# A linear-attention block: reciprocals of the feature sums applied to the values in place of the features

## The chip, the cores and the metric

The kernel runs on one core of a Trainium2 chip. The metric is the device time of one execution in microseconds (us); lower is better. The time before is the median of three runs. One more execution was taken with the hardware profiler; its trace gives the durations used below. The engines are PE (matrix products), ACT, DVE and POOL (elementwise work), and SP, which issues the DMAs. PEld is PE's loading of weights, beside its products.

## The reference

One block: layer norm, linear attention with 16 heads of 28 channels, projection and residual, then layer norm, a gated unit and residual. B is 1, S 2048, D 448, the gated unit is 1792 wide; inputs and outputs are bfloat16.

```python
def _A_ref(x, wqkv, w_phi, wo):
    ...
    pq = jnp.einsum("bhsd,hdf->bhsf", q, w_phi)
    pk = jnp.einsum("bhsd,hdf->bhsf", k, w_phi)
    phi_q = jnp.concatenate([_softmax(pq, axis=-1), _softmax(-pq, axis=-1)], axis=-1)
    phi_k = jnp.concatenate([_softmax(pk, axis=-1), _softmax(-pk, axis=-1)], axis=-1)
    kv = jnp.einsum("bhsf,bhsd->bhfd", phi_k, v)
    z  = jnp.einsum("bhsf->bhf", phi_k)
    num = jnp.einsum("bhqf,bhfd->bhqd", phi_q, kv)
    den = jnp.einsum("bhqf,bhf->bhq", phi_q, z)[..., None] + 1e-6
    o = num / den
    ...
def _B_ref(x, w_gate, w_up, w_down):
    g = jnp.einsum("bsd,df->bsf", x, w_gate)
    u = jnp.einsum("bsd,df->bsf", x, w_up)
    h = _sigmoid(g) * u
    return jnp.einsum("bsf,fd->bsd", h, w_down)
...
x = A_x
h = x + _A_ref(_layernorm(x, axis=-1), A_wqkv, A_w_phi, A_wo)
h2 = h + _B_ref(_layernorm(h, axis=-1), B_w_gate, B_w_up, B_w_down)
```

What matters here: per token, head and sign, the key features are exponentials divided by their sum over 28 channels. `kv` is the sum over all tokens of features times values, `z` the sum of the features. `kv` and `z` need all 2048 tokens before any query can use them.

## The kernel before

**Tiling.** The 2048 tokens are 16 tiles of 128 (t), eight pairs of tiles (pr) and four groups of 512 tokens for the queries (c). The gated unit goes over chunks of 2, 4, 4, 4 and 2 tiles.

**Order.** Every step is a `task` with a name, an engine or a choice of engines, a function that issues its instructions, and the tasks it depends on. A table of numbers, ORDER, gives the order of all tasks: a number divided by 32 is the task, and the remainder picks the engine and, for matrix products, which PSUM banks they fill. `emit` hands each engine its own in-order queue of instructions with semaphore waits: a task waits for what it depends on and for the readers of what its banks held before. TURNS adds a few more waits. So an instruction that waits holds everything that stands behind it on its engine.

**First stage, weights.** SP loads `x`, and the parts of `wqkv` (L474): `Wv`, the key part, and the query part in four pieces called `wq_raw`. `w_phi` is folded into the key and the query weights on the chip. For the queries, two DMA transposes (L513), each reading two of the four pieces, give `WqT`; PE multiplies it with `Wp` (L569, the fold), and copies bring the result to `Wq`. Copies from PSUM share one helper, so `Wk`, `Wq`, `v`, `xnT`, `oT` and `opm` copies all carry line L438.

**Second stage, keys and values.** Per tile: the statistics of the norm (L597 to L607), `xn` (L614 to L618, on DVE, ACT or POOL; ACT's use a small product `nm`, L607), a transpose to `xnT` (SP's DMA transpose L636, or PE for the first tiles with a copy L438), the key and value products into two PSUM banks (L656), the two exponentials `ek` on ACT, a copy of the values `v` with a column of ones beside each head (L438), the sum over channels (`half_s` L686 and the small reduction L692 for the tiles in SPLIT, one large reduction L697 for the others), the reciprocal `rsum` (L701), the features `phi` = `ek` x `rsum` (L703, 896 elements, on DVE or POOL) and 16 `kv` products (L715) that add up in bank 4. `phi` is padded to 32 columns per head, so a weight load has 64 columns. The ones beside the values make the same products give `z`. A product pair takes one of three pairs of banks, (0,1), (2,3) and (6,7); tiles in VV share: two value products fill one pair, two key products another. Between these, the query products (L755) and their exponentials `eq` (L765) are put in.

**Third stage.** `kvz` (L770) takes bank 4 once all 16 tiles are in. Then, per tile, `num` (L791), a copy `opm` (L438), and per pair the division in small steps on DVE and POOL (`rSm` L807, `rr` L809, `b` L811, `c` L814, `rden` L817, `o` L819), the transpose of `o` (`oT`), the product with `wo` (L852), the residual `h` (L882), the second norm (L886 to L896) and its transpose.

**Fourth stage.** Gate and up products (L953), the sigmoid (L962), their product `hh` (L972), down products (L989), the last residual (L996) and the stores (L999). L1009 are products on a bank that nobody reads, put in where PE would be idle.

Of the kernel before, what the change touches and what calls it, by code (L numbers as in the profile page):

```python
# [10 lines left out]
P = 128  # L11
D = 448
# [319 lines left out]
def build(nc, A_x, A_wqkv, A_w_phi, A_wo, B_w_gate, B_w_up, B_w_down, out):  # L332
# [13 lines left out]
    out_t = out[0].rearrange("(n p) d -> p n d", p=P)  # L346
    wd_v = B_w_down.rearrange("(ft p) n -> p ft n", p=P)

    NXP, NEK, NPHI, NV, NOP, NO, NHP, NSG, NSA = 10, 6, 6, 6, 4, 2, 2, 4, 4
    SPLIT = tuple(range(2, 15))  # L350

    with ExitStack() as es:
# [697 lines left out]
```

## Time and profile before

| what | value |
|---|---|
| runs | 203.47, 203.40, 202.22 us; median 203.4 |
| profiled execution | 202.34 us, first to last instruction 200.6 us |
| granted clock of PE, mean | 1.000 |
| DMA | 16.67 MB in 34052 packets, mean 83 GB/s |

A page of the profile counts, for each engine, the time in which it ran instructions. Matrix products are pipelined, so a busy PE can still be held up. The chain of waits follows the work back from the last instruction, at each step to whatever released it. Groups show a line's instructions with their busy time, the mean of one in ns, and the idle time ahead of them. Windows give, for a stretch of the span, each engine's busy time; the columns are named where they are shown.

### The profile page before, as it was taken

How to read it: one execution, taken by the hardware profiler on the slowest of the kernel's cores; microseconds unless marked ns; L12 is line 12 of the kernel's file. 1: busy time of each engine (PE TensorE's matmuls, PEld its weight loads, DVE VectorE, ACT ScalarE, POOL GpSimd, SP SyncE). 2: the span in 40 equal slices, each digit the busy share in tenths (PEclk: the TensorE clock that was granted, in tenths of full speed). 3: DMA queues.
4: the chain of work that ended last, by engine and by line, in shares of the span. 5: the costliest groups of instructions: out<-in, count | busy, mean ns of one | idle time of the engine just before them, and what ended most of it. 6: DMA issues, size and time to landing. Idle time of an engine off the chain costs nothing.

```text
span 200.6 us, 5433 instructions
## 1 busy us (share of the span) xinstructions
PE 195.1 (97%) x2287; PEld 106.5 (53%) x2287; DVE 130.1 (65%) x295; ACT 93.6 (47%) x167; POOL 51.4 (26%) x80
## 2 busy tenths in 40 slices
PE   7999999997999999999999999999999999999994
PEld 2654555555457884444444444555544445785553
DVE  2999999988989999896746942501243345544042
ACT  2699999799997744324242343000002335442000
POOL 6679475460155682540100100100000000000000
DMA  6985589644140460804520004200024000000014
GB/s 186 355 199 115 147 172 269 176 157 137 40 108 3 98 109 21 184 0 101 117 82 0 0 3 54 52 3 0 0 52 137 3 0 3 2 3 3 23 47 159
DMA packets 34052, 16.67 MB, mean 83 GB/s; under 512 B 25644, under 2 KB 33004, under 8 KB 34028
## 3 DMA queue, kind: packets, MB, share of 16 engines
q1 hardware_dynamic: 33676, 16.04, 31.7%
q8 instruction: 18, 0.29, 0.7%
q10 hardware_dynamic: 352, 0.29, 0.4%
q14 instruction: 6, 0.05, 0.1%
HBM read 8.98 MB, written 1.84 MB: 54 GB/s over the span
## 4 chain that ended last, share of the span: by engine, by line
PE 80%; ACT 12%; DVE 2%; POOL 2%; DMA 2%; issue 1%
PE bank L953 42%; PE bank L989 21%; PE bank L656 9%; ACT eq L765 7%; PE bank L852 4%; ACT opm L438 3%; DMA x_sb<-in_A_x_dram 2%; PE bank L715 1%; PE bank L755 1%; DVE st L597 1%; PE bank L791 1%; ACT v L438 1%; POOL rs L602 1%; ACT ek L678 1%; PE bank L569 0%
## 5 line engine op out<-in xcount | busy, mean ns | idle before, releaser
L953 PE MATMUL bank<-xnT,wg_sb 64*128 64x512 bf16 (+1 forms) x490 | 87.3, 333 | 0.0
L953 PE MATMUL bank<-xnT,wu_sb 64*128 64x512 bf16 (+1 forms) x490 | 87.3, 333 | 0.0
L962 ACT ACTIVATE sg_sb<-bank 128x512 f32<-128x512 f32 (+1 forms) x70 | 34.6, 513 | 81.3 <-PE bank L953 76.3
L972 DVE SCALAR_TENSOR_TENSOR hh<-sg_sb,bank 128x512 bf16<-128x512 f32 (+1 forms) x70 | 38.8, 576 | 29.5 <-ACT sg_sb L962 29.5
L953 PEld LDWEIGHTS bank<-xnT,wg_sb 64*128 64x128 bf16 x490 | 45.6, 94 | 19.1 <-issue 0.8
L953 PEld LDWEIGHTS bank<-xnT,wu_sb 64*128 64x128 bf16 x490 | 45.6, 94 | 18.3
L989 PE MATMUL bank<-wd_sb,hh 128*128 128x448 bf16 (+2 forms) x238 | 42.8, 342 | 0.0
L989 PEld LDWEIGHTS bank<-wd_sb,hh 128*128 128x128 bf16 x238 | 22.5, 98 | 20.3 <-issue 0.4
L996 DVE SCALAR_TENSOR_TENSOR x_sb<-bank,x_sb 128x448 bf16<-128x448 f32 (+2 forms) x17 | 9.7, 594 | 29.7 <-PE bank L989 29.7
L656 PE MATMUL bank<-Wk,xnT 64*128 64x448 bf16 x112 | 20.3, 350 | 0.0
L656 PE MATMUL bank<-Wv,xnT 64*128 64x448 bf16 x112 | 20.0, 350 | 0.1
L765 ACT ACTIVATE eq<-bank 128x1024 bf16<-128x1024 f32 x16 | 16.1, 1058 | 0.1
L755 PE MATMUL bank<-xnT,Wq 64*128 64x512 bf16 x112 | 13.6, 376 | 0.0
L852 PE MATMUL bank<-wo_sb,oT 64*128 64x448 bf16 x112 | 13.1, 349 | 0.3 <-ACT eq L765 0.2
L438 ACT CAST opm<-bank 128x960 bf16<-128x960 f32 x14 | 13.0, 982 | 0.2 <-PE bank L791 0.2
L656 PEld LDWEIGHTS bank<-Wk,xnT 64*128 64x128 bf16 x112 | 8.7, 94 | 6.0 <-DMA xnT<-xn_pad 0.9
L686 POOL TENSOR_TENSOR half_s<-ek 128x448 f32<-128x448 bf16 x10 | 9.7, 977 | 6.7 <-DVE phi L703 2.6
L656 PEld LDWEIGHTS bank<-Wv,xnT 64*128 64x128 bf16 x112 | 8.6, 94 | 4.6 <-ACT ek L678 0.6
L892 POOL TENSOR_TENSOR rs<-rs,neghalf 128x2 f32<-128x2 f32 x8 | 5.6, 700 | 19.1 <-DVE rs L890 13.9
L597 DVE BATCH_NORM_STATS2 st<-x_sb 128x6 f32<-128x448 bf16 x16 | 9.0, 610 | 2.2 <-DMA x_sb<-in_A_x_dram 2.1
L882 DVE TENSOR_TENSOR x_sb<-bank,x_sb 128x896 bf16<-128x896 f32 x8 | 8.7, 1092 | 2.6 <-PE bank L852 2.6
L819 POOL TENSOR_TENSOR o_pad<-b_sb,rden 128x896 bf16<-128x896 bf16 x4 | 6.8, 1688 | 13.1 <-DVE rden L817 13.1
(92 smaller groups left out, 198.0 us busy)
## 6 DMA issues: line engine op xcount, KB each, us to landing
wg_sb<-in_B_w_gate_dram SPq DMA_DIRECT2D x4, 448.0 KB, 3.7
wu_sb<-in_B_w_up_dram SPq DMA_DIRECT2D x4, 448.0 KB, 4.3
out_dram<-x_sb SPq DMA_DIRECT2D x15, 112.0 KB, 1.8
wd_sb<-in_B_w_down_dram SPq DMA_DIRECT2D x7, 224.0 KB, 2.8
x_sb<-in_A_x_dram SPq DMA_DIRECT2D x2, 448.0 KB, 5.6
x_sb<-in_A_x_dram SPq DMA_DIRECT2D x3, 224.0 KB, 4.0
wq_raw<-in_A_wqkv_dram SPq DMA_DIRECT2D x4, 128.0 KB, 4.3
Wv<-in_A_wqkv_dram SPq DMA_DIRECT2D x2, 224.0 KB, 4.3
```

The source lines that it names most:

```text
L438: return e.copy(dst, src) if hasattr(e, "activation") else e.tensor_copy(dst, src)
L597: task(("bst", t), "dve", dve(D), lambda e, t=t: e.bn_stats(st1[:, t % 4, :], X(t)), [x_ld[t], opt(("agg", t - 4))])
L656: r = e.matmul(bank[bk][:, 0:D], lhsT=half(xnT, hi)[:, t, k, :], rhs=half(w, hi)[:, k, :], start=(i == 0), stop=(i == 6), tile_position=(6 ...
L686: task(("sa", t), None, 0.88, lambda e, t=t, s=s: e.tensor_tensor(half_s[:, t % NSA].rearrange("p (a n) -> p a n", a=4 * G), ek[:, s].rear ...
L755: r = e.matmul(bank[bb[j]], lhsT=half(Wq2, hi)[:, k, 2 * g:2 * g + 2].rearrange("p c d h -> p (c d h)"), rhs=half(xnT, hi)[:, 4 * c:4 * c ...
L765: task((key, gp, c), "act", act_p(1024), lambda e, gp=gp, c=c, sg=sg, nm=nm: e.activation(eq[c][:, sg, 2 * gp:2 * gp + 2, :], wide[got(nm) ...
L852: r = e.matmul(bank[bb[j]][:, 0:D], lhsT=half(oT, hi)[:, pr % NO, j, k, :], rhs=half(wo_sb, hi)[:, k, :], start=(i == 0 and not res), stop ...
L953: r = e.matmul(bank[b][:, 0:N], lhsT=half(w, hi)[:, k, fs], rhs=half(hnT, hi)[:, t0:t0 + n, k, :], start=(i == 0), stop=(i == 6), tile_pos ...
L962: task(("sig", f_, c), "act", act_p(N), lambda e, j=j, N=N, nm=nm: e.activation(sg_sb[:, j % NSG, 0:N], bank[got(nm)[0]][:, 0:N], ACT.Tanh ...
L972: task(("hh", f_, c), "dve", dve(N), lambda e, j=j, N=N, nm=nm, f_=f_, c=c: e.scalar_tensor_tensor(hhT[c % NHH][:, f_, 0:N], sg_sb[:, j % ...
L989: r = e.matmul(bank[b][:, c0:c1], lhsT=hhT[c % NHH][:, f_, o:o + P], rhs=wd_sb[:, f_, c0:c1], start=(f_ == 0), stop=(f_ == FT - 1))
L996: task(("fin",) + nm[1:], "dve", dve(c1 - c0), lambda e, nm=nm, tt=tt, pr=pr, c0=c0, c1=c1: e.scalar_tensor_tensor(X(tt)[:, c0:c1], bank[g ...
```

## The change

The features are no longer multiplied by the reciprocals of their sums. Since a reciprocal belongs to one token, head and sign, and `kv` sums over tokens, it can be put on the value side: `vs` holds, for each sign, the values of each head times the reciprocal (28 columns) and the reciprocal itself as the 29th column, which takes the place of the ones. The raw exponentials `ek` are now the weights of the `kv` products, 56 columns at a time. The padded `phi`, its two memsets and the ones go; `ek` has eight slots in place of six, `vs` five. Eight tiles (DIRECT) take the values straight from PSUM on DVE, so their value bank is held until the reciprocals are there; the other eight copy them first (`v1`) and scale them on POOL (tiles 0, 1, 5, 9, 12, 13) or DVE (4, 8). VV and SPLIT have other tiles, and ORDER and TURNS are new throughout.

```diff
-224 0 736 96 544 128 1152 256 480 384 576 28512 608 416 160 28800 640 288 28544 800 320 28576 512 352 768
...
+128 288 0 672 480 1088 384 416 512 28192 544 224 160 28256 576 96 256 28512 448 192 736 28416 704 28448 768
...
-    NXP, NEK, NPHI, NV, NOP, NO, NHP, NSG, NSA = 10, 6, 6, 6, 4, 2, 2, 4, 4
-    SPLIT = tuple(range(2, 15))
+    NXP, NEK, NVS, NV, NOP, NO, NHP, NSG, NSA = 10, 8, 5, 4, 4, 2, 2, 4, 4
+    DIRECT = (2, 3, 6, 7, 10, 11, 14, 15)
+    SPLIT = (2, 4, 5, 6, 7, 8, 10, 11, 12, 13)
...
-        task("v1one", "pool", 0.3, lambda e: e.memset(v1[:, :, :, DH:EV], 1.0))
...
-        VV = (0, 2)
+        VV = (0, 2, 6, 10, 14)
...
+            if t not in DIRECT:
+                task(("v1", t), None, act_p(D), lambda e, t=t: copy(
+                    e, v1[:, t % NV, :], bank[got(v_at[t][0])[v_at[t][1]]][:, 0:D]),
...
-            task(("phi", t), None, 1.68, lambda e, t=t, s=s: e.tensor_tensor(
-                phi[:, t % NPHI, :, :, 0:DH, :].rearrange("p a g d h -> p (a g) d h"),
-                ek[:, s].rearrange("p a (g d h) -> p (a g) d h", g=2 * G, h=2),
...
-                [("rs", t), ("ekp", t), ("ekm", t), opt(("kv", t - NPHI))], engs=("dve", "pool"))
+            task(("rs", t), "dve", dve(256), lambda e, t=t, s=s: e.reciprocal(
+                vs[:, t % NVS, :, :, DH], ssum[:, s, :].rearrange("p (a h) -> p a h", a=2)),
+                [("ss", t), opt(("kv", t - NVS))])
+
+            def scaled(e, t=t):
+                v = bank[got(v_at[t][0])[v_at[t][1]]][:, 0:D] if t in DIRECT else v1[:, t % NV, :]
+                return e.tensor_tensor(
+                    vs[:, t % NVS, :, :, 0:DH], v.rearrange("p (h d) -> p h d", d=DH)[:, None, :, :].to_broadcast([P, 2, H, DH]),
+                    vs[:, t % NVS, :, :, DH:EV].to_broadcast([P, 2, H, DH]), ALU.mult)
+            if t in DIRECT:
+                task(("vs", t), "dve", dve(896), scaled, [("rs", t), v_at[t][2]])
+            else:
+                task(("vs", t), None, 1.68, scaled, [("rs", t), ("v1", t)], engs=("pool", "dve"))
...
-                                         lhsT=phi[:, t % NPHI, sg, 2 * g + hi].rearrange("p d h -> p (d h)"),
-                                         rhs=v1[:, t % NV, h:h + 2, :].rearrange("p h e -> p (h e)"), start=False,
+                                         lhsT=ek[:, t % NEK, sg, (2 * g + hi) * 2 * DH:(2 * g + hi + 1) * 2 * DH],
+                                         rhs=vs[:, t % NVS, sg, h:h + 2, :].rearrange("p h e -> p (h e)"), start=False,
```

The order is read at three places. Lines shift: what was L474, L513, L569 and L636 is L470, L509, L565 and L632 in the changed kernel; L807 to L886 become L814 to L893, L438 becomes L436, and L703, the feature product, becomes L708, the value product.

First, SP's queue around the transposes of the query weights, before, where `in_A_wqkv_dram` is the weight tensor in memory:

```order
L474 DMA wq_raw<-in_A_wqkv_dram 128x4x128
L474 DMA wo_sb<-in_A_wo_dram 64x1x448
L474 DMA wq_raw<-in_A_wqkv_dram 128x4x128 x2
L474 DMA wo_sb<-in_A_wo_dram 80x1x448
L513 DMA_TRANSPOSE WqT<-wq_raw 128x8x128 x2
L636 DMA_TRANSPOSE xnT<-xn_pad 128x8x128 x2
```

And the same place on SP in the changed kernel:

```order
L470 DMA wq_raw<-in_A_wqkv_dram 128x4x128 x3
L470 DMA x_sb<-in_A_x_dram 128x4x448
L470 DMA Wv<-in_A_wqkv_dram 128x2x448
L509 DMA_TRANSPOSE WqT<-wq_raw 128x8x128
L470 DMA wq_raw<-in_A_wqkv_dram 128x4x128
L632 DMA_TRANSPOSE xnT<-xn_pad 128x8x128
L509 DMA_TRANSPOSE WqT<-wq_raw 128x8x128
L470 DMA wo_sb<-in_A_wo_dram 16x1x448
L632 DMA_TRANSPOSE xnT<-xn_pad 128x8x128 x3
```

The last piece of `wq_raw` stood ahead of both transposes and now stands behind the first; a transpose of `xn_pad` has come between the two of `WqT`.

Second, PE's queue where the fold of the query weights with `Wp` stands, before:

```order
L656 MATMUL bank<-Wk,xnT 128x448
L656 MATMUL bank<-Wv,xnT 128x448
L569 MATMUL bank<-Wp,WqT 128x112 x12
L656 MATMUL bank<-Wk,xnT 128x448
L656 MATMUL bank<-Wv,xnT 128x448
```

The same place on PE in the changed kernel:

```order
L656 MATMUL bank<-Wk,xnT 128x448 x8
L656 MATMUL bank<-Wv,xnT 128x448 x6
L656 MATMUL bank<-Wk,xnT 128x448 x6
L565 MATMUL bank<-Wp,WqT 128x112 x4
L656 MATMUL bank<-Wk,xnT 128x448
L656 MATMUL bank<-Wv,xnT 128x448
```

The first group of fold products, which was twelve in one row, is four; the rest follow further on. PE's first products in the whole queue were of values and are now of keys.

Third, DVE's queue ahead of the first residual `h` (written to `x_sb`), before:

```order
L817 RECIPROCAL rden<-b_sb 128x32
L438 COPY oT<-bank 128x512
L811 TENSOR_TENSOR b_sb<-opm,rr 128x928
L819 TENSOR_TENSOR o_pad<-b_sb,rden 128x2x448
L814 TENSOR_TENSOR b_sb<-b_sb,opm 128x928
L838 COPY o_pad<-o_pad 128x2x64
L817 RECIPROCAL rden<-b_sb 128x32
L882 TENSOR_TENSOR x_sb<-bank,x_sb 128x896
L886 BN_STATS st<-x_sb 128x6
```

The same place on DVE in the changed kernel:

```order
L845 COPY o_pad<-o_pad 128x2x64
L818 TENSOR_TENSOR b_sb<-opm,rr 128x928
L436 COPY oT<-bank 128x512
L821 TENSOR_TENSOR b_sb<-b_sb,opm 128x928
L814 RECIPROCAL rSm<-opm 128x32
L824 RECIPROCAL rden<-b_sb 128x32
L816 TENSOR_TENSOR rr<-rSm,opm 128x32
L826 TENSOR_TENSOR o_pad<-b_sb,rden 128x2x448
L845 COPY o_pad<-o_pad 128x2x64
L889 TENSOR_TENSOR x_sb<-bank,x_sb 128x896
L893 BN_STATS st<-x_sb 128x6 x2
L889 TENSOR_TENSOR x_sb<-bank,x_sb 128x896
```

Ahead of the first `h` stand now one more product, `o` of the next pair, with its copy, and the small steps of the pair after it; the second `h` follows the first one's statistics at once.

More of the change, by code (lines that the diff above doesn't have):

```diff
@@ L365, in build @@
         a_0, a_1 = nc.lookup_mloc(ek).addr, nc.lookup_mloc(WkT).addr
[L366 to L367 removed]
+        assert nc.lookup_mloc(xn_pad).addr == a_0 + NEK * 2 * D * 2
         assert nc.lookup_mloc(WqT).addr == a_1 + 3 * KT * D * 2 and KT * P >= D
@@ L676, in build @@
             task(("ekp", t), "act", act_p(D), lambda e, t=t, s=s: e.activation(
-                ek[:, s, 0, :], bank[got(k_at[t][0])[k_at[t][1]]][:, 0:D], ACT.Exp), [k_at[t][2], opt(("phi", t - NEK))])
+                ek[:, s, 0, :], bank[got(k_at[t][0])[k_at[t][1]]][:, 0:D], ACT.Exp), [k_at[t][2], opt(("kv", t - NEK))])
             task(("ekm", t), "act", act_p(D), lambda e, t=t, s=s: e.activation(
                 ek[:, s, 1, :], bank[got(k_at[t][0])[k_at[t][1]]][:, 0:D], ACT.Exp, scale=-1.0),
-                [k_at[t][2], opt(("phi", t - NEK))])
-            task(("v1", t), None, act_p(D), lambda e, t=t: copy(
-                e, v1[:, t % NV, :, 0:DH], bank[got(v_at[t][0])[v_at[t][1]]][:, 0:D].rearrange("p (h d) -> p h d", d=DH)),
-                [v_at[t][2], "v1one", opt(("kv", t - NV))], engs=("act", "dve"))
+                [k_at[t][2], opt(("kv", t - NEK))])
+            if t not in DIRECT:
+                task(("v1", t), None, act_p(D), lambda e, t=t: copy(
+                    e, v1[:, t % NV, :], bank[got(v_at[t][0])[v_at[t][1]]][:, 0:D]),
+                    [v_at[t][2]] + [("vs", u) for u in range(t) if u not in DIRECT and u % NV == t % NV][-1:], engs=("act", "dve"))
             if t in SPLIT:
@@ L689, in build @@
                     ek[:, s].rearrange("p a (g n) -> p (a g) n", g=2 * G)[:, :, DH:2 * DH], ALU.add),
-                    [("ekp", t), ("ekm", t), opt(("ss", t - NSA))],
+                    [("ekp", t), ("ekm", t)] + [("ss", u) for u in SPLIT if u < t and u % NSA == t % NSA][-1:],
                     engs=("pool", "dve"))
@@ L899, in build @@
                     [("rstd2", pr), h_of.get(t)] + [d for d in hT_of.get(pr - NHP, [])])
-            qdone = [("q", gp, c) for gp in range(2)] + [("pb", NT - 1)]
+            qdone = [("q", gp, c) for gp in range(2)] + [k_at[NT - 1][2]]
             if pr in PE_O:
```

27 lines of the change are left out of this document (11 added, 16 removed), and 99 rows, old and new, of tables (ORDER, TURNS).

## The prediction

> **What bounds the kernel now.** The page comes first: span, busy shares, and the chain of waits by engine.
>
> ```profile
> span 200.6 us, 5433 instructions
> PE 195.1 (97%) x2287; PEld 106.5 (53%) x2287; DVE 130.1 (65%) x295; ACT 93.6 (47%) x167; POOL 51.4 (26%) x80
> PE 80%; ACT 12%; DVE 2%; POOL 2%; DMA 2%; issue 1%
> ```
>
> The profiled execution took 202.34 us, 1.74 us more than its span. A busy PE may still be starved, so the chain in order of time comes second.
>
> ```profile
> 24.22 1.13 PE bank L715 x64
> ...
> 33.43 4.65 PE bank L656 x48
> 38.08 0.86 PE bank L755 x8
> ...
> 41.72 4.79 ACT eq L765 x5
> 46.51 4.31 ACT opm L438 x5
> ...
> 61.91 0.23 PE bank L791 x16
> ...
> 62.71 3.49 PE bank L953 x64
> ...
> 123.27 26.59 PE bank L989 x140
> ...
> 181.82 16.05 PE bank L989 x98
> ```
>
> PE carries it up to 39 us, ACT's exponentials and `opm` copies follow, and PE has it again from the first gate/up products (62.7 us) to the end. Third come the windows: per engine its busy time and instructions, then clock, DMA share and GB/s.
>
> ```profile
> 20.00:30.00 10.00, 10.00 (x158) 5.24 (x154) 9.81 (x21) 9.90 (x21) 6.08 (x9) 1.00 0.73 159
> 30.00:39.50 9.50, 9.50 (x177) 5.22 (x174) 9.25 (x20) 8.19 (x18) 4.80 (x5) 1.00 0.83 219
> 39.50:45.00 5.50, 5.48 (x135) 3.16 (x130) 4.67 (x9) 5.47 (x8) 3.33 (x2) 1.00 0.51 170
> 45.00:62.50 17.50, 15.95 (x310) 8.77 (x311) 16.23 (x38) 17.47 (x21) 4.33 (x4) 1.00 0.31 82
> 62.50:90.00 27.50, 27.50 (x414) 17.76 (x412) 26.24 (x72) 12.77 (x27) 15.26 (x13) 1.00 0.36 76
> ```
>
> PE has no gap from 20 to 45 us and none from 62.5 us on; between, 1.55 us are open. The granted clock is 1.00. So two things set the end: when the key/value stage lets `kvz` be formed, and how long after it the gate/up products start. The rest is a fixed row of PE work. DVE (9.81 of 10) and ACT (9.90 of 10) are as full as PE in the first stage, so relief of one alone brings little.
>
> **The change part by part.** *DVE up to `kvz`.* Groups by shape: busy us, mean ns.
>
> ```profile
> L703 DVE TENSOR_TENSOR phi<-ek,rsum 128x896 bf16<-128x896 bf16 x14 | 9.4, 705 | 0.1
> L882 DVE TENSOR_TENSOR x_sb<-bank,x_sb 128x896 bf16<-128x896 f32 x8 | 8.7, 1092 | 2.6 <-PE bank L852 2.6
> L618 DVE TENSOR_SCALAR xn_pad<-x_sb,mv,rs 128x512 bf16<-128x512 bf16 x6 | 2.2, 390 | 0.2 <-POOL rs L602 0.2
> L686 DVE TENSOR_TENSOR half_s<-ek 128x448 f32<-128x448 bf16 x3 | 1.8, 614 | 0.0
> L692 DVE TENSOR_REDUCE ssum<-half_s 128x32 f32<-128x448 f32 x13 | 7.7, 605 | 0.3
> L697 DVE TENSOR_REDUCE ssum<-ek 128x32 f32<-128x896 bf16 x3 | 3.1, 1033 | 0.0
> L438 DVE CAST Wq<-bank 128x448 bf16<-128x448 f32 x1 | 0.6, 614 | 0.0
> L438 ACT CAST v<-bank 128x448 bf16<-128x448 f32 x14 | 7.2, 543 | 0.5 <-PE bank L715 0.4
> L615 ACT ACTIVATE xn_pad<-x_sb,nm,rs 128x512 bf16<-128x512 bf16 x4 | 3.2, 810 | 0.9 <-POOL nm L607 0.9
> ```
>
> Removed: 14 feature products (9.4 us), four `xn` (4 x 0.37 = 1.5), two half sums (1.2), three small reductions that become large ones (3 x 0.59 = 1.8), the `Wq` copy (0.6): 14.5 us. Added: eight products straight from PSUM. The trace has none; the nearest row of the same size that reads PSUM is L882 (1.09 us), the lower bound is the feature product from SBUF (9.4/14 = 0.67). I take 1.09, as it reads the same bank type and count: 8.7 us. Two value products from SBUF on DVE (tiles 4 and 8), between 0.67 and 1.09, middle 0.9: 1.8 us. Three large reductions: 3.1 us; one more `xnT` copy and two tiny `nm` products, 0.6 us by estimate. Sum 14.2, so DVE gains 0.3 us, with ends from a gain of 4.1 (0.67 for all ten) to a loss of 0.1 (1.09 for all ten). It is not relieved. One wait is new: a reciprocal writes into one of five value slots and waits for the `kv` matmuls of the tile five back. Behind it on DVE stand the next sums and products, and PE waits for those. PE issues `kv` of tile 10 ahead of two query groups (28 products at 0.86/8, 3.0 us) and of the last five `kv`, so I cost it at nothing; uncovered it is a part of rival C.
>
> The Trainium skill, "VectorE: DVE Perf Modes", section "The perf-mode tier table (the rule you actually need)", speaks against this edit: a two-tensor operation handles two elements a cycle from bf16 SBUF operands, but one with any PSUM operand. By it (0.96 GHz there) eight products of 896 elements cost an estimated 3.7 us more than the ones removed; by the two rows it is 8 x (1.09 - 0.67) = 3.4 us.
>
> *ACT.* It loses eight value copies (8 x 0.51 = 4.1 us) and gains two `xn` (1.6), one `Wq` copy against one `xnT` copy (nothing): 2.5 us free before its row of `opm` copies. But those need `kvz`, so the gain only waits, unless `kvz` comes earlier. *POOL* takes four more long products and two more `xn`, about 8 us; it was busy 6.08 + 4.80 + 3.33 = 14.2 of 25 us from 20 to 45 us, and the gaps hide them. *PE*: 56 weight columns in place of 64; no row shows a difference, taken as nothing. Two memsets that POOL did during the first loads go, at no gain. The `wd` loads move behind seven more transposes on SP; the first down products stand at 123 us, and the gate/up products ahead of them hide it; without that cover each microsecond of delay would be one of time.
>
> *SP and the fold of the query weights.* The four `wq_raw` pieces went out before the first transposition; now the last piece stands behind it. Issues first, then the times to landing of `wq_raw` and of `WqT`, then the page's busy tenths of DMA.
>
> ```profile
> 8.39 1.13 SPq L474 DMA_DIRECT2D wq_raw<-in_A_wqkv_dram  x2
> ...
> 12.57 3.30 SPq L513 DMA_TRANSPOSE WqT<-wq_raw  x2
> ```
> ```profile
> DMA to landing us min/median/max: 3.2/4.0/4.9
> ```
> ```profile
> DMA to landing us min/median/max: 3.2/3.5/3.7
> ```
> ```profile
> DMA  6985589644140460804520004200024000000014
> ```
>
> The third piece goes out at about 8.4 us as before (12 issues ahead of it, then 13), so the first transposition again starts at 12.6 us and takes half of 3.30. The last piece goes out at 14.2 us. DMA is emptier there (8, then 5 tenths, against 9), so I take its shortest landing, 3.2: 17.4 us. Then the second transposition, 3.5 to landing: 20.9 us (ends 20.6 and 22.8). Who waits is PE, whose fold matmuls need both halves, and behind them the whole row of value and query products. When does PE get there?
>
> ```profile
> 9.09 1.95 ACT L438 CAST Wk<-bank 128x448 bf16<-128x448 f32 x4
> ```
> ```profile
> 10.56 0.93 PE L656 MATMUL bank<-Wv,xnT 64*128 64x448 bf16 x8
> 18.99 0.76 PE L569 MATMUL bank<-Wp,WqT 112*128 112x112 bf16 x12
> ```
>
> Before, PE began with value products at 10.56 us; now it begins with key products, which need the folded `Wk` (copies end at 11.04): 11.2 us, a loss of 0.6. Then come 84 products at 4.65/48 = 0.097 us (8.15) and eight transposes (0.6 by estimate): 19.9 us. It waits 1.0 us (ends 0.6 and 2.9). The transposes of `xn_pad` behind it on SP go out about 1.5 us before PE needs them. As PE has no gap from 20 to 45 us, `kvz` comes 0.6 + 1.0 = 1.6 us later.
>
> *After `kvz`.*
>
> ```profile
> 45.02 0.64 DVE L770 TENSOR_TENSOR kvz<-bank,dmask 128x464 bf16<-128x464 f32 x1 [0.79 <-PE bank L715]
> ...
> 54.52 1.09 DVE L882 TENSOR_TENSOR x_sb<-bank,x_sb 128x896 bf16<-128x896 f32 x1
> ...
> 59.74 1.09 DVE L882 TENSOR_TENSOR x_sb<-bank,x_sb 128x896 bf16<-128x896 f32 x1 [0.39 <-PE bank L852]
> 60.75 0.74 DVE L438 COPY xnT<-bank 128x512 bf16<-128x512 bf16 x2
> ```
>
> Before, `kvz` to the first `h` took 9.5 us, to the end of the `xnT` copies 16.5, to the first gate/up products 17.5 (PE is full from 62.5 on). Five more DVE rows now stand ahead of the first `h`, one product and four small ones, 1.6 us by the sizes above; the second `h` moves ahead of the norm (1.0), where it stood ahead of the copies (1.0). The copies end 18.0 us after `kvz`, the products start at 18.1: 0.6 later. Two more groups of 16 `num` matmuls (0.23 each) are then done ahead of them: 0.5 back. Net 0.1. The tail from the down products on stands in the same order.
>
> Sum: 0.6 + 1.0 + 0.1 = 1.7 us, 202.34 to 204.0. The profiled execution lies 1.1 below the median of the three runs (203.4), so on their scale I forecast 205.1.
>
> **The rivals.** *A, nothing nets (0.25).* The fold is covered: PE is late itself, because ACT (9.90 of 10) frees its banks late. Then the start costs 0.6 at most and the rest 0.1: 203.4 to 204.1, say 203.8. For: the lower end of the wait is only 0.6. Against: the fold needs three DMA steps in a row, and PE had no gap here.
>
> *B, faster (0.10).* DVE is freed of a lock.
>
> ```profile
> L703 DVE TENSOR_TENSOR phi<-ek,rsum x14: 559/615/1385, 21.0 to 43.6; 128x896 bf16<-128x896 bf16 x14
> ```
> ```profile
> 21.32 1.06 POOL L686 TENSOR_TENSOR half_s<-ek 128x448 f32<-128x448 bf16 x1
> ```
>
> The product of 1.385 us ran beside this POOL sum and ended with it; unhindered it takes 0.56. If the PSUM products run free of POOL and near 0.67, DVE gains 4.1 us and this 0.8, and `kvz` comes as soon as PE allows: 224 products at 0.097 (21.7 us), 256 `kv` matmuls at 1.13/64 (4.5), 56 query products at 0.86/8 (6.0), folds and transposes 1.6 by estimate, 33.8 us from 11.2 on, which is 45.0, no earlier than before. What is then left to win is the 1.55 us that PE has open behind it and the 0.46 of the `num` groups: 203.4 - 2.0 = 201.4. It decides if a PSUM product takes under 0.8 us and the chain behind `kvz` fills PE. Against: L882. The Trainium skill, "SBUF — State Buffer", section "Who interferes with whom", says that a DVE instruction with two SBUF inputs contends with a GpSimd instruction that reads SBUF, and one with a single SBUF input outside the two-port modes does not; the PSUM products have one. The 1.385 us agree with the rule.
>
> *C, banks held (0.20).* A value pair must stay in PSUM until two sums, two reciprocals (0.3 each, by estimate half a reduction) and two products are done on DVE: 2 x (0.59 + 0.3 + 1.09) = 4.0 us, where PE fills the other two pairs in 2 x 14 x 0.097 = 2.7. Three such pairs have a successor in the stage: 3 x 1.3 = 4 us, 207.4. For: DVE is full. Against: key products are now issued ahead, so sums are ready early. That the change does not do what it says is excluded: the DVE row shows eight products that read `bank`.
>
> **How the numbers follow.** Forecast 0.45 (203.8 to 207), A 0.25 (203 to 204.5), B 0.10 (200.4 to 202.4), C 0.20 (206 to 209). About 1% (2.0 us) can be told from no change. Faster than 201.4: half of B and a rest for what I did not see, 0.08. Slower than 205.4: C and about half of the forecast, 0.43. Same: 0.49. The range runs from 201.4 to 208.3: it leaves out half of B and the upper third of C, and some for what I did not see.
>
> **What would show it.** Right: the second fold group on PE starts near 21 us behind a DMA wait, DVE's PSUM products take 1.0 to 1.1 us, `kvz` starts near 46.6, the first gate/up product near 64.3, and PE is full behind it. Wrong: `kvz` at 45 or earlier with no DMA wait on PE (A or B), or PE waiting for DVE products ahead of value products (C).

## The result, and the profile after

The changed kernel took 205.65 us (median of four runs, 205.41 to 206.03) against 202.97 us (four runs), a ratio of 1.013 with an interval of 1.010 to 1.017: slower by 2.7 us, inside the range and half a microsecond from the number forecast. The profiled execution took 205.85 us, 3.5 more than that of before, which was itself 0.6 below its median.

The page of the changed kernel, its span, busy shares and the chain by engine:

```profile
span 203.9 us, 5406 instructions
PE 197.1 (97%) x2287; PEld 109.5 (54%) x2287; DVE 129.9 (64%) x286; ACT 92.9 (46%) x161; POOL 58.7 (29%) x82
PE 76%; ACT 9%; DVE 6%; POOL 3%; DMA 3%; issue 1%; ACTq 0%; POOLq 0%
```

DVE has as much to do as before (129.9 against 130.1 us), POOL 7.3 us more, and DVE, POOL and DMA have larger shares of the chain (6, 3 and 3% against 2% each). Where that is, the chain of the changed kernel in order of time shows (start, duration, engine):

```profile
15.94 1.09 DVE ssum L698
...
21.59 1.94 DVE vs L708 x2
23.81 0.97 POOL half_s L687
24.78 0.98 POOL rs L598
26.34 0.81 ACT xn_pad L611
...
29.97 3.47 DMA xnT<-xn_pad
33.49 4.90 PE bank L656 x50
...
46.39 1.05 PE bank L722 x64
47.46 0.65 DVE kvz L777
48.60 6.14 ACT opm L436 x7
...
65.24 2.90 PE bank L960 x50
```

Before, PE carried the chain through the key/value stage; now it runs from DVE's and POOL's sums through the norm of the last four tiles (`rs`, `xn_pad`), their transposition, and PE. `kvz` starts at 47.46 us against 45.02, the first gate/up product at 65.24 against 62.55. The windows of the changed kernel (columns as in the prediction):

```profile
20.00:30.00 10.00, 9.29 (x162) 5.00 (x160) 8.55 (x16) 9.10 (x20) 9.40 (x12) 1.00 0.25 48
30.00:39.50 9.50, 9.34 (x164) 5.14 (x161) 9.23 (x18) 6.18 (x11) 8.48 (x7) 1.00 0.89 162
39.50:45.00 5.50, 5.50 (x68) 2.53 (x64) 5.36 (x10) 4.43 (x7) 2.76 (x2) 1.00 0.56 166
```

From 20 to 30 us every engine is open at some time: PE 0.71 us, DVE 1.45 us (before 0.19). POOL has become the fullest, 9.40 of 10 against 6.08. From 30 us on ACT has room too (6.18 of 9.5, before 8.19). PE is full from 39.5 to 45 us in both.

So of the 3.5 us, PE's first product starts 0.49 later (11.05 against 10.56); from there to `kvz`, which I call PE's row below, it takes 36.41 us against 34.46, 1.95 more; from `kvz` to the first gate/up product 17.78 against 17.53, 0.25 more; from there to the last instruction 0.6 more (138.6 against 138.0); 0.2 lies outside the span. Single executions spread by some tenths here: the last stretch took 138.2 us in e9 and e10, which have the changed order, and 138.4 in e3, which has the old one.

The windows over the whole row, before and changed:

```profile
10.56:45.02 34.46, 34.30 (x562) 18.44 (x560) 33.13 (x77) 32.45 (x64) 22.82 (x33) 1.00 0.72 174
11.05:47.46 36.41, 35.43 (x561) 18.37 (x560) 33.72 (x66) 30.54 (x56) 29.98 (x36) 1.00 0.62 142
```

With the same products to do, PE is open for 0.8 us more (0.98 against 0.16) and counted as busy for 1.1 us more (35.43 against 34.30).

### The profile page after: what moved, and what is told of

The parts are those of the page before. It is cut to its first block, busy times and chain, and to the rows that moved or that the text cites. A ratio compares the mean times of both kernels' runs of the same rounds, so it can differ in the third digit from the quotient of the medians.

```text
span 203.9 us, 5406 instructions
## 1 busy us (share of the span) xinstructions
PE 197.1 (97%) x2287; PEld 109.5 (54%) x2287; DVE 129.9 (64%) x286; ACT 92.9 (46%) x161; POOL 58.7 (29%) x82
## 4 chain that ended last, share of the span: by engine, by line
PE 76%; ACT 9%; DVE 6%; POOL 3%; DMA 3%; issue 1%; ACTq 0%; POOLq 0%
PE bank L960 42%; PE bank L996 21%; PE bank L859 4%; ACT opm L436 3%; PE bank L656 3%; PE bank L762 3%; ACT eq L772 2%; DMA xnT<-xn_pad 2%; DMA x_sb<-in_A_x_dram 2%; DVE ssum L698 1%; POOL rs L598 1%; ACT ek L676 1%; ACT ek L678 1%; PE bank L722 1%; DVE st L593 1%
## 5 line engine op out<-in xcount | busy, mean ns | idle before, releaser
L656 PE MATMUL bank<-Wk,xnT 64*128 64x448 bf16 x112 | 17.1, 350 | 0.4 <-DMA xnT<-xn_pad 0.2
L656 PE MATMUL bank<-Wv,xnT 64*128 64x448 bf16 x112 | 16.8, 350 | 0.0
L762 PE MATMUL bank<-xnT,Wq 64*128 64x512 bf16 x112 | 14.6, 377 | 0.3 <-ACT opm L436 0.2
L436 ACT CAST opm<-bank 128x960 bf16<-128x960 f32 x15 | 13.5, 981 | 2.0 <-PE bank L798 1.9
L818 POOL TENSOR_TENSOR b_sb<-opm,rr 128x928 bf16<-128x928 bf16 x4 | 7.0, 1742 | 18.7 <-DVE o_pad L845 17.1
L897 POOL TENSOR_SCALAR rs<-mv 128x2 f32<-128x2 f32 x6 | 1.2, 193 | 38.1 <-DVE mv L895 32.3
L708 POOL TENSOR_TENSOR vs<-v,vs 128x896 bf16<-128x896 bf16 x6 | 11.0, 1837 | 3.8 <-DVE vs L702 3.8
L678 ACT ACTIVATE ek<-bank 128x448 bf16<-128x448 f32 x16 | 8.5, 552 | 3.5 <-PE bank L656 3.5
L656 PEld LDWEIGHTS bank<-Wk,xnT 64*128 64x128 bf16 x112 | 6.6, 94 | 6.0 <-PE bank L656 0.5
```

Source lines behind the costliest of these rows:

```text
L436: return e.copy(dst, src) if hasattr(e, "activation") else e.tensor_copy(dst, src)
L656: r = e.matmul(bank[bk][:, 0:D], lhsT=half(xnT, hi)[:, t, k, :], rhs=half(w, hi)[:, k, :], start=(i == 0), stop=(i == 6), tile_position=(6 ...
L678: task(("ekm", t), "act", act_p(D), lambda e, t=t, s=s: e.activation(ek[:, s, 1, :], bank[got(k_at[t][0])[k_at[t][1]]][:, 0:D], ACT.Exp, s ...
L708: return e.tensor_tensor(vs[:, t % NVS, :, :, 0:DH], v.rearrange("p (h d) -> p h d", d=DH)[:, None, :, :].to_broadcast([P, 2, H, DH]), vs[ ...
L762: r = e.matmul(bank[bb[j]], lhsT=half(Wq2, hi)[:, k, 2 * g:2 * g + 2].rearrange("p c d h -> p (c d h)"), rhs=half(xnT, hi)[:, 4 * c:4 * c ...
```

## The experiments

All times are medians; each is set against runs of the kernel before on the same chip. "Row" is the time from PE's first product of keys or values to `kvz` in the profiled execution.

| run | what | us | before | ratio (95%) | first product, `kvz` | row |
|---|---|---|---|---|---|---|
| before | | 202.97 | | | 10.56, 45.02 | 34.5 |
| changed | | 205.65 | 202.97 | 1.013 (1.010 to 1.017) | 11.05, 47.46 | 36.4 |
| e1 | last `wq_raw` piece early | 206.20 | 202.87 | 1.017 (1.013 to 1.021) | 10.88, 47.41 | 36.5 |
| e2 | arithmetic alone, old order | 210.11 | 202.87 | 1.036 (1.032 to 1.039) | 10.35, 51.50 | 41.2 |
| e3 | the same, by head pairs | 202.59 | 202.87 | 0.999 (0.997 to 1.001) | 11.38, 46.08 | 34.7 |
| e4 | no value straight from PSUM | 210.48 | 202.87 | 1.037 (1.033 to 1.040) | 10.98, 52.43 | 41.5 |
| e5 | changed, by head pairs | 204.99 | 202.61 | 1.013 (1.008 to 1.018) | 11.06, 47.01 | 36.0 |
| e6 | changed, one sign | 205.97 | 202.61 | 1.015 (1.011 to 1.018) | 11.06, 47.9 | 36.8 |
| e7 | `kv` in five groups | 205.86 | 202.61 | 1.015 (1.012 to 1.018) | 11.04, 47.8 | 36.8 |
| e8 | e5, e7 and relief at the end | 209.22 | 202.61 | 1.028 (1.021 to 1.036) | 10.95, 48.9 | 38.0 |
| e9 | `Wv` early | 205.42 | 202.44 | 1.015 (1.013 to 1.017) | 10.84, 47.36 | 36.5 |
| e10 | one sign, `Wv` early | 205.88 | 202.44 | 1.017 (1.014 to 1.020) | 10.85, 47.01 | 36.2 |
| e11 | pairs, `Wv` early, relief | 208.72 | 202.44 | 1.031 (1.028 to 1.035) | 10.81, 48.63 | 37.8 |
| e12 | e5, e7 and e9 together | 205.54 | 202.89 | 1.015 (1.011 to 1.018) | 11.96, 48.58 | 36.6 |

### e1: the last piece of the query weights early

SP's queue in the changed kernel, and the edit:

```diff
 L470 DMA Wv<-in_A_wqkv_dram 128x2x448
+L470 DMA wq_raw<-in_A_wqkv_dram 128x4x128
 L509 DMA_TRANSPOSE WqT<-wq_raw 128x8x128
-L470 DMA wq_raw<-in_A_wqkv_dram 128x4x128
 L632 DMA_TRANSPOSE xnT<-xn_pad 128x8x128
```

> The changed kernel, with one edit: on SP the last piece of wq_raw is issued ahead of the first transposition, as it was before the change. The forecast's theory (PE waits 1.0 us for the second transposition): the kv sum closes 1.0 us earlier, kvz at 46.5 us, time 204.6. The rival read from the trace of the changed kernel (the fold groups at 20.2 and 24.0 us show no wait on a DMA; what is late is work on POOL and DVE): nothing changes, kvz at 47.5 +- 0.2, time 205.6 +- 0.4.

`kvz` moved by 0.05 us and the time not down. The forecast's wait is not there, and PE's timeline of the changed kernel had already said so; the two fold groups, with no idle time ahead of them:

```profile
20.21 0.37 PE L565 MATMUL bank<-Wp,WqT 112*128 112x112 bf16 x4
...
23.98 0.76 PE L565 MATMUL bank<-Wp,WqT 112*128 112x112 bf16 x12
```

SP's timeline of the changed kernel shows why. It got to the transposition 1.2 us sooner than before (11.34 against 12.57):

```profile
11.34 1.35 SPq L509 DMA_TRANSPOSE WqT<-wq_raw  x1
12.73 0.57 SPq L470 DMA_DIRECT2D wq_raw<-in_A_wqkv_dram  x1
14.90 1.24 SPq L632 DMA_TRANSPOSE xnT<-xn_pad  x1
16.24 1.27 SPq L509 DMA_TRANSPOSE WqT<-wq_raw  x1
```

I had put the last piece's issue at 14.2 us and its landing at 17.4; it went out at 12.73, and the second transposition was issued at 16.24. The shorter of the two transpositions' times to landing is 2.8 us, which gives 19.0 for the second one; PE came to its first fold at 20.21.

### e2 and e3: the arithmetic without the new order

e2 is the kernel before with its order and its engines, where only the feature product becomes a value product. Its innermost dimension is the channel, and the reciprocal is repeated along it, as in the change:

```diff
-            task(("phi", t), None, 1.68, lambda e, t=t, s=s: e.tensor_tensor(
-                phi[:, t % NPHI, :, :, 0:DH, :].rearrange("p a g d h -> p (a g) d h"),
...
+            task(("vs", t), None, 1.68, lambda e, t=t: e.tensor_tensor(
+                vs[:, t % NVS, :, :, 0:DH],
+                v1[:, t % NV, :].rearrange("p (h d) -> p h d", d=DH)[:, None, :, :].to_broadcast([P, 2, H, DH]),
+                vs[:, t % NVS, :, :, DH:EV].to_broadcast([P, 2, H, DH]), ALU.mult),
```

In e3 the innermost dimension is the pair of heads, and the reciprocal is repeated one dimension further out; the copy of the values, the `kv` products and `kvz` follow that layout:

```diff
-                vs[:, t % NVS, :, :, 0:DH],
-                v1[:, t % NV, :].rearrange("p (h d) -> p h d", d=DH)[:, None, :, :].to_broadcast([P, 2, H, DH]),
-                vs[:, t % NVS, :, :, DH:EV].to_broadcast([P, 2, H, DH]), ALU.mult),
+                vs[:, t % NVS, :, :, 0:DH, :],
+                v1[:, t % NV, :].rearrange("p (a d h) -> p a d h", d=DH, h=2)[:, None].to_broadcast([P, 2, 2 * G, DH, 2]),
+                vs[:, t % NVS, :, :, DH:EV, :].to_broadcast([P, 2, 2 * G, DH, 2]), ALU.mult),
```

(In both, `ek` has eight slots, `vs` six, the copies of the values have no ones, and two small constants share the memory of a later buffer.)

> The kernel before, its order, engines and sharing of banks kept, with the new arithmetic alone: values copied, then scaled by the reciprocals (value product in place of the feature product on the same engine), raw exponentials as weights. Theory A (the price of the product): the trace of the changed kernel has the product from SBUF at 1.03 us against 0.62 for the feature product; 14 on DVE are 5.7 us on an engine that is busy 9.8 of 10 us, so kvz moves from 45.0 to 48.5 to 50.7 us and the time to 206.5 to 208.7. Rival B (the new order costs, the arithmetic does not): kvz at 45.0 +- 0.3, time 203.0 +- 0.5.

> As e2_arith, but values and scaled values lie with the two heads of a pair innermost, as the features did (channel, then head), so the product has the operands' shapes of the feature product. Theory A (the product's price comes from its layout, a reciprocal repeated along the innermost dimension, not from the source): 0.56 to 0.70 us per product, kvz at 45.0 +- 0.4, time 203.0 +- 0.6. Rival (the price comes from two operands with a broadcast, in whatever layout): about 1.03 us per product, time as e2_arith.

The value products by group (min/median/max in ns, first and last start), e2 first:

```profile
L700 DVE TENSOR_TENSOR vs<-v,vs x14: 1028/1081/1855, 20.8 to 49.7; 128x896 bf16<-128x896 bf16 x14
```
```profile
L700 DVE TENSOR_TENSOR vs<-v,vs x14: 565/614/1394, 21.9 to 45.0; 128x896 bf16<-128x896 bf16 x14
```

Same engine, same elements, same source: 1.08 us with the repeated reciprocal innermost, 0.61 with the pair innermost, and that is the feature product's 0.615. In e2, PE's waits say who it waits for:

```profile
PE bank L712 <- DVE vs L700: 3.2, 6, 0.8
PE bank L712 <- POOL vs L700: 2.1, 2, 1.1
```

e2 loses 6.7 us in PE's row and 1.3 behind it (PE's clock fell near the end of the row, last section). e3 is level with the kernel before, with a row of 34.7 us. So the arithmetic costs nothing in the right layout, and 7 us in the layout of the change if the order is the old one. In the new order, with the same innermost dimension, the changed kernel loses 2.7.

### e4: copies in place of products from PSUM

```diff
-    NXP, NEK, NVS, NV, NOP, NO, NHP, NSG, NSA = 10, 8, 5, 4, 4, 2, 2, 4, 4
-    DIRECT = (2, 3, 6, 7, 10, 11, 14, 15)
+    NXP, NEK, NVS, NV, NOP, NO, NHP, NSG, NSA = 10, 8, 5, 6, 4, 2, 2, 4, 4
+    DIRECT = ()
```

> The changed kernel with no value taken straight from PSUM: the eight tiles are copied by ACT as soon as their product is done (six slots for copies), and scaled on DVE from SBUF; all else in the same order. Theory A (a product costs DVE the same from PSUM and from SBUF, and banks are not what is short): products 1.03 us in place of 1.08, ACT 4.3 us more, kvz 47.5 to 48.5 us, time 205.6 to 206.6. Rival C (value banks held until the reciprocals are there delay PE): kvz 1 to 2 us earlier, time 203.7 to 204.7.

Both expectations fell: `kvz` came 5 us later. The products in the changed kernel:

```profile
L708 DVE TENSOR_TENSOR vs<-bank,vs x8: 1022/1076/1095, 21.5 to 45.9; 128x896 bf16<-128x896 f32 x8
L708 POOL TENSOR_TENSOR vs<-v,vs x6: 1714/1719/2432, 18.4 to 43.9; 128x896 bf16<-128x896 bf16 x6
L708 DVE TENSOR_TENSOR vs<-v,vs x2: 1033/1396/1759, 26.6 to 35.3; 128x896 bf16<-128x896 bf16 x2
```

And in e4:

```profile
L708 DVE TENSOR_TENSOR vs<-v,vs x10: 1028/1410/2607, 21.8 to 50.8; 128x896 bf16<-128x896 bf16 x10
L708 POOL TENSOR_TENSOR vs<-v,vs x6: 1720/1722/2608, 18.5 to 48.2; 128x896 bf16<-128x896 bf16 x6
```

Undisturbed, a product takes 1.02 to 1.10 us from either source. But from SBUF it took up to 2.6 us, while from PSUM 1.10 is the longest of eight, six of which ran beside a product or sum of POOL. The changed kernel's own slow one shows beside what, and who waited for it; three rows of its timeline:

```profile
26.39 2.75 POOL L687 TENSOR_TENSOR half_s<-ek 128x448 f32<-128x448 bf16 x2 [0.34 <-DVE nm L603]
26.55 1.76 DVE L708 TENSOR_TENSOR vs<-v,vs 128x896 bf16<-128x896 bf16 x1
...
28.37 0.41 PE L722 MATMUL bank<-vs,ek 128*56 128x58 bf16 x16 [0.53 <-DVE vs L708]
```

Two half sums take POOL 1.9 us otherwise, and here both engines lost 0.7 to 0.8; PE's sum of that tile waited 0.53 for the product. PE's waits in e4 up to `kvz` show further prices, ACT's eight copies and a load (e6):

```profile
PE bank L656 <- ACT v L436: 2.1, 2, 1.1
PE bank L656 <- DMA Wv<-in_A_wqkv_dram: 1.3, 1, 1.3
PE bank L762 <- ACT ek L678: 1.0, 1, 1.0
PE bank L722 <- DVE vs L708: 0.8, 2, 0.6
```

They are 5.2 us, and the row is 5.0 longer than the changed kernel's: ACT, with its eight copies more, has 3.1 of them, DVE's products directly 0.8. Since ACT's copies came in with the edit, e4 says little on rival C, banks held for too long. The waits of the changed kernel itself say more; up to `kvz` there are two:

```profile
PE bank L722 <- DVE vs L708: 0.5, 1, 0.5
PE bank L656 <- DMA xnT<-xn_pad: 0.2, 1, 0.2
```

No wait for a bank is among them, where rival C wants 4 us.

### e5, e6, e10: a cheaper product in the new order

e5 lays copied and scaled values out by pairs as in e3; a product from PSUM becomes two, one for each sign:

```diff
+                if t in DIRECT:
+                    for sg in range(2):
+                        r = e.tensor_tensor(
+                            vs[:, t % NVS, sg, :, 0:DH, :],
+                            bank[got(v_at[t][0])[v_at[t][1]]][:, 0:D].rearrange("p (a h d) -> p a d h", d=DH, h=2),
+                            vs[:, t % NVS, sg, :, DH:EV, :].to_broadcast([P, 2 * G, DH, 2]), ALU.mult)
+                    return r
```

> The changed kernel in its own order, with copied values and scaled values laid out by head pairs (the two heads innermost), as in e3. A value product straight from PSUM is then two instructions, one for each sign. Theory A (layout sets the price from SBUF, PSUM keeps its own): the two DVE products from SBUF fall from 1.4 to 0.6 us, the PSUM products cost 2 x 0.6 = 1.2 in place of 1.08; DVE gains 1.6 and loses 1.0 us, kvz 47.0 to 47.5, time 205.2 to 205.7. Rival (layout sets the price from PSUM too): a PSUM product takes 0.7 us in all, DVE gains 4.5 us, kvz 46.0, time 204.

```profile
L709 DVE TENSOR_TENSOR vs<-bank,vs x16: 559/612/625, 21.5 to 45.6; 128x448 bf16<-128x448 f32 x16
L714 DVE TENSOR_TENSOR vs<-v,vs x2: 565/934/1302, 26.5 to 34.8; 128x896 bf16<-128x896 bf16 x2
```

As theory A has it: from PSUM half a product takes 0.61 us in the new layout, so a whole one 1.2, no less than the 1.08 before; from SBUF the layout brings 1.03 down to 0.565 in the faster of the two. `kvz` came 0.45 us earlier; the ratio to the kernel before stayed at 1.013.

e6 leaves the minus sign's product out for the ten tiles on DVE:

```diff
+                if t in HALF:
+                    return e.tensor_tensor(
+                        vs[:, t % NVS, 0, :, 0:DH], v.rearrange("p (h d) -> p h d", d=DH),
+                        vs[:, t % NVS, 0, :, DH:EV].to_broadcast([P, H, DH]), ALU.mult)
...
-                                         rhs=vs[:, t % NVS, sg, h:h + 2, :].rearrange("p h e -> p (h e)"), start=False,
+                                         rhs=vs[:, t % NVS, 0 if t in HALF else sg, h:h + 2, :].rearrange("p h e -> p (h e)"), start=False,
```

> The changed kernel in its own order, with the ten value products on DVE done for the plus sign alone; the kv products of the minus sign of these tiles read the plus sign's values. So half of each product is left out, and nothing else. DVE has 10 x 0.5 = 5 us less to do. Theory A (DVE's products hold the kv sum back): kvz 1.0 to 1.5 us earlier (46.0 to 46.5), time 204.2 to 204.7. Rival (PE's own work, its start and its order set kvz): kvz within 0.3 us of 47.5, time 205.4.

It told nothing on that, as a wait came in that the changed kernel's profile doesn't have: PE waited 1.6 us for `Wv`. The new order issues the second piece of `Wv` at 9.2 us (9.6 in e4 and e6), where it stood at 3.9. In the seven profiles with that order of loads (the changed kernel, e1, e4 to e8) its landing lies at the edge of the first value products at 14.4 us: PE waits 0.9 to 1.6 us for it in e4, e6 and e7, and 0.2 at most in the other four. So e10 repeats e6 with that load back at its old place.

> e6 (the ten value products on DVE done for the plus sign alone, the minus sign's kv products of these tiles read the plus sign's values) with the second piece of Wv issued early as in e9, since e6 lost 1.63 us to that load. Theory A (DVE's products hold the kv sum back in the changed kernel): kvz 46.0 to 46.4, time 204.2 to 204.6. Rival (they don't): kvz 47.2 to 47.6, time 205.2 to 205.6.

`kvz` at 47.01, between the two. With 4.3 us less on DVE (29.6 us busy in the row against 33.9), PE's row is 0.36 us shorter than in e9, which is e10 with whole products; the median times, 205.88 and 205.42 us, show no gain. And DVE now waits for PE ahead of `kvz`; its row in the changed kernel, then in e10:

```profile
47.46 0.64 DVE L777 TENSOR_TENSOR kvz<-bank,dmask 128x464 bf16<-128x464 f32 x1 [0.51 <-PE bank L722]
```
```profile
47.01 0.64 DVE L782 TENSOR_TENSOR kvz<-bank,dmask 128x464 bf16<-128x464 f32 x1 [1.88 <-PE bank L727]
```

0.51 us is what PE needs for the last sums; in e10, DVE had been done 1.4 us earlier and it helped little. DVE's products are a limit in the changed kernel, but PE's row is another one, 0.4 us behind it.

### e7, e9, e12: PE's breaks and the load

In the changed kernel PE forms the `kv` sum in eight groups, before in four (e7's text counts nine, as the wait of 0.53 us splits one of them in the timeline). e7 makes it five, by moving tile 0 to 1 and 2, tiles 3 and 4 behind the value products of 6 and 7, 8 and 9 to 10, 11 to the last four.

> The changed kernel with the kv products gathered on PE: tile 0 with 1 and 2, tiles 3 and 4 behind the next value products, 8 and 9 with 10, 11 with 12 to 15; five groups in place of nine. In the trace a group of 16 costs PE 0.17 us beyond its products. Theory A (DVE's last products set the end of the kv sum, the last of them ends at 46.9 us): kvz 0 to 0.3 us earlier, time 205.4 to 205.7. Rival (PE's breaks set it): 4 x 0.17 and the wait of 0.53 us at tile 4 go, kvz 1.0 us earlier, time 204.6.

e9 moves the load of `Wv` alone:

```diff
-L470 DMA Wv<-in_A_wqkv_dram 128x2x448
+L470 DMA Wv<-in_A_wqkv_dram 128x2x448 x2
 L470 DMA wo_sb<-in_A_wo_dram 112x1x448
...
 L470 DMA x_sb<-in_A_x_dram 128x4x448
-L470 DMA Wv<-in_A_wqkv_dram 128x2x448
 L509 DMA_TRANSPOSE WqT<-wq_raw 128x8x128
```

> The changed kernel with one edit on SP: the second piece of Wv is issued right behind the first, as before the change, in place of 9.2 us. Theory A (in the changed order this load lands at the edge of PE's first value products, in the profile of the changed kernel in time, in three of the other profiles of its order 0.9 to 1.6 us late, and DVE's and POOL's work behind takes most of such a delay up): no wait of PE for Wv, kvz 47.2 to 47.5 us, time 205.2 to 205.6, that is 0 to 0.4 less than the changed kernel. Rival (most of the loss is this load): time 203.5 to 204.3.

e12 has the pair layout, the groups and the load:

> The changed kernel with three of the edits together: the layout by head pairs (e5), the kv products in five groups (e7) and the second piece of Wv early (e9). Theory A (in the changed kernel two limits lie within half a microsecond of each other, DVE's products and PE's row with its breaks, so that each edit alone gains at most 0.5 us and both together gain more): kvz 46.2 to 46.6 us, time 204.0 to 204.6. Rival (the edits don't add, the rest of the order holds it): kvz 47.0, time 205.0 to 205.4.

e7 lost 0.9 us to `Wv`, and its row of 36.8 us would have been 35.9 if all of that had come off, which nothing shows. e9 came out as expected, level with the changed kernel: the late load is not the loss. By e12 the gains don't add: its median is level with the changed kernel's, its row 36.6 us. Its profiled execution, 206.79 us, lies 1.25 above its median, and its `kvz` at 48.58 has a late start in it, 0.9 us after the changed kernel's. So the five groups did not shorten PE's row; the 0.7 us that the rival in e7 counted for four breaks did not come off.

### e8 and e11: relief at the end, misjudged

Tiles 14 and 15 copied by ACT, half sums of 13 to 15 on POOL; in e11 the products of 12 and 13 move from POOL to DVE.

> e5 and e7 together, and relief for DVE at the end of the stage: tiles 14 and 15 are copied by ACT and scaled from SBUF, their sums and that of tile 13 begin with a half sum on POOL. DVE has 0.6 + 2 x 0.4 + 2 x 0.5 = 2.4 us less among the last rows. Theory A: kvz 1.0 to 1.8 us earlier than in the changed kernel (45.7 to 46.5), time 203.9 to 204.7. Rival (the start at 11.05 us and PE's work hold it): kvz 47.0, time 205.2.

> The changed kernel with the layout by head pairs, the second piece of Wv early, and relief at the end: tiles 14 and 15 copied by ACT, the products of tiles 12 to 15 on DVE from SBUF at 0.6 us, their sums begun with half sums on POOL. Theory A: kvz 46.0 to 46.6, set by PE (start at 11.05 us, 33.6 us of work, 1.5 to 2 us of breaks), time 203.8 to 204.5. Rival (the order after kvz has room and PE's breaks go too): 202.5 to 203.3, level with the kernel before.

In both the products of 14 and 15 ran on POOL, not on DVE as e11's text says, and PE waited for them. From the waits of e11:

```profile
PE bank L729 <- POOL vs L714: 1.5, 2, 1.3
```

So e8 and e11 show that two products on POOL at the end of this stage make PE wait (1.72 us each, the second from 46.4 us on in e11), and nothing on the relief that was meant.

No version beat the kernel before; e3 equals it.

## Why the prediction was right, and where it was not

**The number.** 205.1 forecast, 205.65 measured. The forecast's own step was further off: it put the change at 1.7 us, and measured are 2.7 between the medians and 3.5 between the two profiled executions. (With a fourth run the median of before is 202.97, where the forecast stood on 203.4.) Of the sum's three terms the first held, the largest did not come, and the third came out small, but not by its reasons. Of its signs two held, the price of a product from PSUM and PE being full behind the first gate/up product; the DMA wait was not there, and `kvz` and the first gate/up product came 0.9 us later than it said.

**The start, 0.6 forecast.** PE begins with key products, which need the folded `Wk`: 0.49 us later. The step is in the trace: the weight load of the first key product waits 0.5 us for `Wk`, whose last copy ends at 10.82. The size is less sure, as single executions spread: 10.35 to 11.38 us in the three profiles of the old order, 10.8 to 11.1 in those of the new one, with 11.96 in e12.

**The fold, 1.0 forecast: wrong.** "The last piece goes out at 14.2 us", and so "It waits 1.0 us", failed. The piece went out at 12.73, PE found both transpositions done, and e1, which undoes the edit, gains nothing. The step took the time of the first transposition from the kernel before, though I had counted the issues ahead of it; SP had 1.2 us less to wait there.

**In its place** stand 1.95 us that PE's row is longer. "As PE has no gap from 20 to 45 us, `kvz` comes 0.6 + 1.0 = 1.6 us later" took the row itself as unchanged. What the runs showed of it: leaving out half of each product on DVE is worth 0.36 us (e10 against e9), the layout by pairs 0.45 (e5, in which PE's wait of 0.53 us at tile 4 is gone); the load of `Wv` nothing in the median (e9). e3 against e5 shows the rest from the other side: same arithmetic, same layout for what comes from SBUF, and the old order has a row of 34.7 us, the new one 36.0.

Where these microseconds lie, the starts of PE's products tell. Rows of the changed kernel's timeline:

```profile
38.32 0.64 PE L722 MATMUL bank<-vs,ek 128*56 128x58 bf16 x32
38.89 0.74 PE L656 MATMUL bank<-Wk,xnT 64*128 64x448 bf16 x6
...
40.42 0.41 PE L722 MATMUL bank<-vs,ek 128*56 128x58 bf16 x16
40.77 0.82 PE L762 MATMUL bank<-xnT,Wq 64*128 64x512 bf16 x6
41.43 0.92 PE L656 MATMUL bank<-Wv,xnT 64*128 64x448 bf16 x8
...
45.56 0.82 PE L762 MATMUL bank<-xnT,Wq 64*128 64x512 bf16 x6
46.32 1.10 PE L722 MATMUL bank<-vs,ek 128*56 128x58 bf16 x64
```

From start to start, six query products take 0.66 us when value products follow and 0.76 when `kv` products follow. Sixteen `kv` products take 0.35 and thirty-two 0.57, so 0.13 is there once per group, however large it is. Key, value and query products have weights of 64 rows (64*128 in these lines), `kv` products, transposes and folds of 112 or 128 (128*56 here); a change from one kind to the other costs about 0.1 us either way, and the profile counts it as busy. Up to `kvz` PE makes 21 such changes, before 11: about 1.0 of the 1.95 us. The two waits listed under e4, 0.53 and 0.16 us, are most of the rest. e3, with the old order's 11 changes, and e5, with 21, differ by 1.25 us in the row. That a kernel with fewer changes would be faster is not shown: e12 makes 15, but its waits for transposes of `xn` are 0.6 us in place of 0.16, further short stalls came in, and the row is no shorter. DVE, POOL and the transposes of `xn`, through which the chain now runs, stand close behind PE, and what the order would have to change for both was not tried.

**DVE, a gain of 0.3 forecast.** In the row DVE is busy 33.72 us against 33.13: 0.6 more. The price from PSUM was right (1.09 taken, 1.08 measured). The price from SBUF was not: 0.9 taken, 1.03 undisturbed and 1.76 beside POOL. I took a middle between two rows, and the row that it should have been near was L882, for a reason that I had not looked at: which dimension is innermost. The Trainium skill, "VectorE: DVE Perf Modes", section "What auto-detection actually checks", has it: two elements a cycle are taken only if every tensor is 16-bit with step 1 or -1. With the reciprocal repeated innermost its step is 0. By e2 and e3 the rule holds: 1.03 against 0.565 us for the fastest of each. In the prediction I had quoted the table of that page alone, which speaks of where the operands lie; by it the two products from SBUF would have cost what the feature product does, an estimated 0.6 us.

**After `kvz`, 0.1 forecast**: 0.25 to the first gate/up product (17.78 against 17.53 us; e5, e9, e10 and e12 have 17.8 too). The net was near, its two parts were not. The five more DVE rows put the first `h` 1.5 us later behind `kvz`, as forecast (1.6), but the `xnT` copies end 17.6 us behind it where 18.0 was forecast, and the products 17.8 in place of 18.1. And the 0.5 us that should come back was misread from the order: 192 `num` products stand ahead of the first gate/up product in both kernels, not two groups more. (The sign "near 64.3" does not follow from the working either; 46.6 + 18.1 is 64.7.)

**The rivals.** *A*: the fold is covered, as it said, but its time was 203.8, as it had nothing for PE's row. *B*: its lock is there. Products from PSUM ran free of POOL (at most 1.10 us, against up to 2.6 from SBUF in e4). But the products stayed at 1.08 us, above the 0.8 from which it decides, and PE's row was the limit in any case. The product of 1.385 us that it shows did not end with POOL's sum, though: it ran from 21.49 to 22.87 us, and the sum ended at 22.38, so it was held while the sum ran and then took its usual half microsecond. The Trainium skill, "SBUF — State Buffer", section "Who interferes with whom", says that a DVE instruction with two SBUF inputs contends with a GpSimd instruction that reads SBUF, and one with a single SBUF input outside the two-port modes does not. Both kinds of rows agree with it. What the new order gains back of the 7 us of e2 is not this alone: DVE is busy 39.6 us in e2's row and 33.7 in the changed kernel's, with six products on POOL in place of two. *C*: has no support, as no wait for a bank is listed (under e4).

So the forecast's size was right with one term of 1.0 us that wasn't there and 1.95 us in its place that I had not seen. Nothing in the working gave the second; that the total came out is in that part luck, and the median of before moved 0.4 us the right way.

## What to carry to other kernels

Before costing an elementwise product, look at which dimension is innermost in every operand: a factor that is repeated along it made the product 1.03 us in place of 0.565, and swapping two dimensions took it back at no cost. Where the other operand came straight from PSUM, the product was no faster, but POOL's work beside it did not hold it up. When an order is changed, count how often PE changes from one form of product to another: here each change cost about 0.1 us, though taking some of them away again (e12) gained nothing, as other waits took their place. To judge a change that comes with a new order, run its arithmetic in the old order: here that took two runs, and showed a price of 7 us for the layout (in the old order) and none for the idea; the new order with the better layout (e5) is 2.4 us slower than the kernel before.

## What the runs showed of the hardware that I had not expected

PE's clock falls without PE ever being idle for long. In e2, at the end of the stage (windows; the last three columns are clock, DMA share and GB/s):

```profile
46.00:48.00 2.00, 0.82 (x46) 0.61 (x38) 1.97 (x5) 2.00 (x4) 2.00 (x2) 1.00 0.76 229
48.00:50.00 2.00, 0.54 (x22) 0.44 (x24) 1.97 (x4) 1.01 (x2) 0.87 (x1) 0.94 0.00 0
50.00:51.00 1.00, 0.59 (x22) 0.46 (x22) 0.81 (x1) 0.00 (x0) 0.00 (x0) 0.50 0.06 16
...
56.00:57.00 1.00, 1.00 (x8) 0.37 (x6) 1.00 (x5) 0.77 (x1) 0.00 (x0) 0.71 0.82 216
57.00:58.00 1.00, 1.00 (x26) 0.61 (x24) 0.91 (x2) 0.35 (x1) 0.00 (x0) 1.00 0.06 12
```

At the end of 4 us in which PE was busy a third of the time, in pieces with waits of 1.1 us at most, the granted clock fell, and it was 0.50 for 6 us, until PE had been full for some 3 us. The 1.3 us that e2 loses behind `kvz` lie ahead of its first gate/up product (18.84 us against 17.53), where this stretch is. e11 had the same: PE busy 0.68 of 2 us from 46 us on, the clock 0.73 over the next 2 us, then 0.50 from 50 to 52. The Trainium skill, "TensorE: Matmul & The Clock Gate", section "What's actually happening", tells of half clock after an idle window of about 3.4 us. In e2 PE was never idle for that long ahead of the fall.

The two pieces of `Wv`, 224 KB each, took 4.2 to 6.6 us to land in the seven profiles with one order of loads. An order that leaves this load no slack came through without a wait in four of these profiles and waited up to 1.6 us in the other three.
